# Attention and mixture of experts on one core: regrouping the small loads of the second weights, and phi in longer packets

## The chip, the cores and the metric

The kernel runs on one core of one Trainium2 chip, in one launch. The metric is the device time of that core in microseconds (us), the median of several runs. The core has five engines that run side by side: PE (TensorE, matrix products and transposes), ACT (ScalarE), DVE (VectorE), POOL (GpSimd) and SP (SyncE, which here only issues DMAs). DMAs are issued from the queues of POOL, SP and ACT and are carried out by 16 DMA engines. SBUF is the on-chip memory of 128 partitions, PSUM the small memory that PE writes to.

## The reference

The program is a sliding-window attention followed by a soft mixture of experts. Cut to what matters:

```python
# attention: 8 batches, 8 heads, 576 positions, head size 64
scores = (q @ k.T) / 8
mask_plain = (rel >= 0) & (rel < 32)                         # heads 0-3
mask_dil = (rel >= 0) & (rel < 128) & (rel % 4 == 0)         # heads 4-7
attn = softmax(where(mask, scores, -1e9)); x = attn @ v      # -> 4608 tokens x 512
# soft mixture of experts: phi 512 x 32, w1 8 x 512 x 1024, w2 8 x 1024 x 512
logits = x @ phi                                             # 4608 x 32 slots
d = softmax(logits, over tokens); slot_input = d.T @ x       # 32 slots, 4 per expert
for e in range(8):
    h = relu(slot_input[e] @ w1[e])
    slot_out[e] = h @ w2[e]
c = softmax(logits, over slots); out = c @ slot_out          # 4608 x 512
```

All inputs and the output are float32 in HBM.

## The kernel before

**Units.** The attention is done in eight units, u = 0 to 7, each of one pair of batches and one half of the heads (dilated for even u, plain for odd u). A unit's q, k and v are loaded by `load_unit` into one of three buffers, `stg[:, u % 3]`, of 9,216 bfloat16 columns: q in partitions 0 to 31, k in 32 to 63, v in 64 to 95. Even units take three DMAs that write 32 adjacent partitions each, odd units six that write every second partition of 32. `st_T` turns the unit round by PE transposes into `TT` (two buffers), `st_S` makes the scores and their exponentials, `st_V` and `st_P` multiply with v and normalize into `XB`, `st_X` transposes `XB` into `XT` (L767, six transposes of 96 x 128 for each half x of the 256 columns of a head kind), and `st_L` makes the logits with phi (`phi_pad`, which is cast from `phi_st`) and adds up the slots' inputs.

**Weights.** Weights are cast from float32 to bfloat16 by the loading DMA, all from POOL's queue. `home` gives each expert matrix a place: w1 of experts 0 to 6 in `WD`; w1 of expert 7 and w2 of expert 0 in `stg[:, 2]`, w2 of experts 1 and 2 in `stg[:, 0]`, of experts 3 and 4 in `stg[:, 1]`, each in 4,096 columns, the second of a buffer from column 4096 on; w2 of experts 5 to 7 in `TT`. A weight can be loaded when the attention has finished with the buffer. One expert's w2 takes 4,096 columns in each of 128 partitions: 16 KB of float32 in HBM for a row, 8 KB of bfloat16 in SBUF.

**The loads in question.** Experts 1 and 2 come in one DMA of all 128 rows (`wload2`, L495). For experts 3 and 4, `wpair` issues seven DMAs over both experts: rows 0, 2, 4 ... 126; rows 1, 9, 17 ... 41; rows 49 and 57; rows 65, 73 ... 105; rows 113 and 121; rows 5, 13 ... 125; and rows 3, 7, 11 ... 127. [...] Behind them in the queue come expert 5 (`wload("w25")`), a memset of `hTT` by POOL, and experts 6 and 7 in seven parts, cut into halves of the columns.

**The end.** When the attention is through, the slots' inputs are folded, the first products (`pe` with `siT`) and the second (`ffn2`) run, the second half by half as weights land: `ffn2` takes experts 0 to 3 in its first call, 4 to 6 in part in the next, and 6 and 7 last, first for output columns 0 to 255, then for 256 to 511. `half` makes the output of 1,536 tokens for each half of the columns and stores it in pieces; after it the other tokens follow in four larger stores. Output is staged in the weights' places in `WD` and `stg[:, 2]`.

**Order.** `Prog.schedule` orders the work of all engines by planned times, cost estimates and keys (`DUE`); operations of POOL and of SP keep the order in which the program lists them. `Prog.emit` then writes each engine's list with its semaphore waits. A buffer's `Buf` object keeps who wrote and read it, and `b.parts` which DMA brings which part of a weight, so that a product waits for the parts that it reads.

**phi.** SP issues the load of phi at the start, behind an early load of part of w1: `phi_st` is 128 partitions x 4 x 32 float32, and partition p takes rows p, 128 + p, 256 + p and 384 + p of phi, 128 bytes each.

Of the kernel before, what the change touches and what calls it, by code (L numbers as in the profile page):

```python
# [25 lines left out]
QB = 96  # L26
# [30 lines left out]
class Op:  # L57
    n = 0
# [58 lines left out]
class Prog:  # L117
# [6 lines left out]
    def op(self, e, fn, r=(), w=(), a=(), alloc=(), cost=0.5, key=0.0, mode="f",  # L124
           sem=None, nbytes=0, after=(), ndma=1, n=0, port=False):
        o = Op(e, fn, cost, key, mode)
        deps = list(after)
        for b in r:
            deps += b.ready
        for b in w:  # L130
            b.fresh()
            deps += b.prev
        for b in a:
            deps += b.prev
        seen = set()
        for d in deps:
            if d.id not in seen:
                seen.add(d.id)
                o.deps.append(d)
        for b in r:  # L140
            b.reads.append(o)
        for b in list(w) + list(a):
            b.ready.append(o)
        o.wr = [b for b in list(w) + list(a) if b.pool is not None]
        for b in list(r) + list(w) + list(a):
            if b.pool is not None and b not in o.touch:
                b.left += 1
                o.touch.append(b)
        o.alloc = list(alloc)
        o.sems = sem  # L150
        o.bytes = nbytes
        o.ndma = ndma
        o.n = 2 * n
        o.port = port
        self.ops.append(o)
        return o
# [171 lines left out]
def bass_dilated_sliding_attn__then__soft_moe_slots_kernel(  # L328
# [12 lines left out]
    op = P.op  # L341

    def sb(name, shape, dt=BF16):
        return A(nc.sbuf_tensor(name, shape, dt))
# [3 lines left out]
    WD = sb("WD", [128, 7, 4096])  # L348
    stg = sb("stg", [128, 3, 9216])
# [11 lines left out]
    ident = sb("ident", [128, 128])  # L361
# [4 lines left out]
    phi_st = sb("phi_st", [128, 4, N_SLOTS], F32)  # L366
# [26 lines left out]
    def tile(pool, size=1):  # L393
        t = Buf(pool)
        t.size = size
        return t
# [5 lines left out]
    def sbt(t):  # L402
        return t.pool.ts[t.phys[0]]
# [7 lines left out]
    def bankb(t):  # L411
        return psb[:, t.phys[0], :]
# [5 lines left out]
    b_stg = [Buf() for _ in range(3)]  # L418
# [7 lines left out]
    def due(u, x):  # L426
        return u * DUE["pace"] + x

    def kind(u):
        return 1 - u % 2  # L430
# [23 lines left out]
    HOME = {}  # L454
    b_home = []

    def home(ap, al, name):
        b = Buf()
        b.al = al
        b.parts = []  # L460
        HOME[name] = (ap, b)
        b_home.append((ap, b))
# [24 lines left out]
    def wload2(na, nb):  # L487
        (ap, ba), (_, bb) = HOME[na], HOME[nb]
        e = int(na[2:])
        src = (moe_w1 if na[:2] == "w1" else moe_w2)[e:e + 2].rearrange("e (p c) f -> p e (c f)", p=128)  # L490
        dst = WD[:, e:e + 2, :] if na[:2] == "w1" else stg[:, 0, 0:8192].rearrange("p (e f) -> p e f", e=2)
        pb = Buf()
        for al in ba.al + bb.al:
            pb.prev = pb.prev + al.ready + al.reads
        o = op("pool", lambda g: [g.dma_start(dst, src)], after=pb.prev, a=[pb], cost=0.8,  # L495
               sem=DmaSem(nc, f"s_{na}_{nb}"), nbytes=4194304)
        for b in (ba, bb):
            b.parts.append((0, 8, 0, 512, pb))
            b.ready.append(o)
# [4 lines left out]
    for i, s in enumerate((2, 0, 1)):  # L504
        for h_ in range(2):
            nm = ("w17", "w20", "w21", "w22", "w23", "w24")[2 * i + h_]
            home(stg[:, s, 4096 * h_:4096 * h_ + 4096], [b_stg[s]], nm)
    TTf = TT[:].rearrange("p a x -> p (a x)")
    for i in range(3):
        home(TTf[:, 4096 * i:4096 * i + 4096], b_TT, f"w2{5 + i}")  # L510
# [5 lines left out]
    op("sp", lambda e: [e.dma_start(  # L516
        pre, moe_w1[0].rearrange("(p c) f -> p (c f)", c=4)[:, 0:2048])],
       w=[b_pre], cost=0.1, sem=DmaSem(nc, "s_pre"), nbytes=1048576)
    op("sp", lambda e: [e.dma_start(phi_st[:], moe_phi.rearrange("(c p) s -> p c s", p=128))],
       w=[b_phist], cost=0.1, sem=s_phi, nbytes=65536)  # L520
    op("dve", lambda g: g.memset(id0[:], 0.0), w=[b_id0], cost=0.3)
    op("pool", lambda g: g.affine_select(out=id0[:], in_=id0[:], compare_op=AluOp.not_equal,
# [60 lines left out]
    def blocked(u):  # L583
        return u > 0 and kind(u) == 0
# [170 lines left out]
    def st_X(u, bpar, x):  # L755
        bp, ty = u // 2, kind(u)
        b = 2 * bp + bpar
        px = tile(psum, 1)
        al = [px]
        if x == 0:  # L760
            XT[b, ty] = tile(pXT)
            al.append(XT[b, ty])
        xt, xb = XT[b, ty], XB[b, ty]

        def pe(t):
            for m in range(6):
                i_ = t.transpose(bankb(px)[:, QB * m:QB * m + QB],  # L767
                                 sbt(xb)[:, m, 128 * x:128 * x + 128], ident[0:QB, 0:QB])
            return i_
        k0 = due(u, DUE["X"] + DUE["Xb"] * bpar + 0.8 * x)  # L770
        op("pe", pe, r=[b_id, xb], w=[px], alloc=al, cost=0.31, n=6, key=k0)

        def ev(en):
            d, s_ = sbt(xt)[:, x, :], bankb(px)[:, 0:S]
            if ty:
                s_ = s_.rearrange("p (y x s) -> p s x y", y=2, x=2)
                d = d.rearrange("p (s x y) -> p s x y", y=2, x=2)
            if en is nc.vector:
                return en.tensor_copy(d, s_)
            return en.activation(d, s_, ACTF.Copy)  # L780
        op(("dve", "act"), ev, r=[px], **{"w" if x == 0 else "a": [xt]},
           cost={"dve": 0.38 if ty == 0 else 0.8, "act": 0.57}, key=k0 + 0.6)
# [59 lines left out]
            return i_  # L842
        op("pe", pe3, r=[et, xb0, xb1], a=[b_acc, t_acc], cost=0.35, n=12, mode="c", key=k0 + 4.0)

    mk = sb("mk", [15, 5, 2, 4])
    turns = []

    def turn(n):
        i = len(turns)
        turns.append(n)  # L850
        op("pool", lambda g: [g.dma_start(
            mk[0:n, i, :, 0:2],
            moe_w2[7, 0:n, :].rearrange("p (a x) -> p a x", a=4)[:, 0:2, 0:2])],
           w=[Buf()], cost=0.3, sem=DmaSem(nc, f"s_turn{i}"), nbytes=256)

    def wpair(na, nb, s_, steps):
        e0 = int(na[2:])
        bs = [HOME[na][1], HOME[nb][1]]
        v_ = moe_w2[e0:e0 + 2].rearrange("e (p c) f -> p e (c f)", c=8)
        d_ = stg[:, s_, 0:8192].rearrange("p (e f) -> p e f", e=2)  # L860
        for n, st in enumerate(steps):
            if isinstance(st, int):
                turn(st)
                continue
            r0, r1, step = st
            pb = Buf()
            for al in bs[0].al:
                pb.prev = pb.prev + al.ready + al.reads
            src, dst = v_[r0:r1:step], d_[r0:r1:step]
            o = op("pool", lambda g, src=src, dst=dst: [g.dma_start(dst, src)],  # L870
                   after=pb.prev, a=[pb], cost=0.6, sem=DmaSem(nc, f"s_{na}_{n}"),
                   nbytes=32768 * ((r1 - r0 + step - 1) // step))
            for b in bs:
                b.parts.append((0, 8, 0, 512, pb))
                b.ready.append(o)

    W_AFTER = {2: ["w10"], 3: ["w11"], 4: ["w12"], 5: ["w13"], 6: ["w14"]}
    for u in range(NU):
        for j in range(4):
            st_T(u, j)  # L880
        if u + 3 < NU:
            for n_ in W_AFTER.get(u + 2, ()):
                wload(n_, ((4, 8, 0, 512),) if n_ == "w10" else ((0, 8, 0, 512),))
            load_unit(u + 3)
        else:
            if u == 5:
                wload2("w15", "w16")
                wload("w17")
                wload("w20")
            if u == 6:  # L890
                wload2("w21", "w22")
            if u == 7:
                wpair("w23", "w24", 1, (
                    (0, 128, 2), 15, (1, 49, 8), 2, (49, 65, 8), 6, (65, 113, 8), 2,
                    (113, 128, 8), 7, (5, 128, 8), (3, 128, 4)))
        if u + 1 < NU and blocked(u + 1):
            interleave(u + 1)
        for i in range(6):
            st_S(u, i)
        for g in range(4):  # L900
            st_V(u, g)
        for g in range(4):
            st_P(u, g)
        for bpar in range(2):
            for x in range(2):
                st_X(u, bpar, x)
        if u % 2:
            for bpar in range(2):
                st_L(u - 1 + bpar, u)
# [79 lines left out]
    COLS, d_ = [], 0  # L989
# [3 lines left out]
    for x in range(2):  # L993
        def rsum(t, x=x):
# [5 lines left out]
           cost=0.8, key=K1 + x, after=[ffn1] if x else [])  # L1000
    op("dve", lambda vv: vv.reciprocal(rtok[:], bank(rs)[:, 0:N_TOK // 128]), r=[rs], w=[b_rtok],
       cost=0.2, key=K1 + 1)
# [200 lines left out]
```

## Time and profile before

| | us |
|---|---|
| Median of three runs | 175.43 (175.20 to 175.62) |
| The profiled execution, its own time | 175.14 |
| Its span, first to last instruction | 173.9 |
| PE busy | 127.0 (73%) |
| DVE busy | 113.8 (65%) |
| ACT busy | 95.9 (55%) |
| POOL busy | 62.8 (36%) |
| Mean granted TensorE clock | 0.929 of full speed |
| DMA packets | 12,517, 41.28 MB |

The profile is of one execution. Times are us from the start of the span. Its page has the busy time of each engine, the span in 40 equal slices (a digit is the busy share of a slice in tenths, 9 is 90% or more; the DMA row is the mean over the 16 DMA engines, and the GB/s row is what they moved), the DMA queues, the chain of waits that ended last, the costliest groups of instructions, and the DMA issues with their time from issue to landing. "L495" is line 495 of the kernel; a name like `stg<-in_moe_w_dram` is destination and source. A DMA's issue on POOL is an instruction of its own; the transfer goes on after it.

### The profile page before, as it was taken

The page shows a single profiled execution, that of the slowest core. Times are in us where ns is not written, and L with a number is a line of the kernel's source. Part 1 is how long each engine was busy: PE and PEld are TensorE (multiplying, and loading weights), DVE is VectorE, ACT ScalarE, POOL GpSimd, SP SyncE. Part 2 cuts the span into 40 slices and gives each one's busy share as a digit, 9 for nine tenths or more (in the row PEclk, how much of TensorE's full clock was granted, in tenths as well). Part 3 has the DMA queues.
Part 4 walks back from the last instruction along what each step waited for, and adds up shares of the span by engine and source line. Part 5 has one row for each costly group of instructions (what it writes and reads, how often), then busy time and mean ns, then how long its engine had stood idle before and what let it go on. Part 6 is the DMA issues. An engine that isn't in the chain of part 4 may idle for free.

```text
span 173.9 us, 5097 instructions
## 1 busy us (share of the span) xinstructions
PE 127.0 (73%) x2235; PEld 97.3 (56%) x2235; DVE 113.8 (65%) x259; ACT 95.9 (55%) x147; POOL 62.8 (36%) x106
## 2 busy tenths in 40 slices
PE   0003778987889999979899799987879896599000
PEld 0003758976678877858787688666553533353000
DVE  6960079769978899886979978999430301489400
ACT  2310791789868878776888587674301101589300
POOL 6950199500996006762001756809700000000000
PEclk9999996999999999999999999999975999969755
DMA  5999999999999999998999999999999999999998
GB/s 170 273 208 197 218 231 196 215 212 214 228 212 207 216 214 209 245 212 189 219 214 216 213 215 220 213 215 219 213 211 209 206 197 196 294 358 396 422 433 351
DMA packets 12517, 41.28 MB, mean 237 GB/s; under 512 B 2128, under 2 KB 8784, under 8 KB 9040
## 3 DMA queue, kind: packets, MB, share of 16 engines
q0 software_dynamic: 7952, 30.41, 86.9%
q1 hardware_dynamic: 2912, 8.98, 13.3%
q10 hardware_dynamic: 1632, 1.57, 2.7%
q8 instruction: 17, 0.28, 0.6%
q14 instruction: 4, 0.03, 0.0%
HBM read 61.93 MB, written 9.44 MB: 410 GB/s over the span
## 4 chain that ended last, share of the span: by engine, by line
PE 35%; DMA 23%; DVE 21%; ACT 7%; POOL 4%; issue 3%
DMA TT<-in_moe_w_dram 15%; DMA stg<-in_v_dram 8%; PE ps L641 7%; PE ps L635 6%; DVE XB L750 6%; PE ps L710 6%; DVE PT L700 4%; PE ps L685 4%; ACT TT L667 3%; PE ps L739 3%; PE ps L794 3%; POOL TT L481 3%; PE ps L767 3%; DVE WD L1058 3%; ACT PT L692 3%
## 5 line engine op out<-in xcount | busy, mean ns | idle before, releaser
L692 ACT ACTIVATE PT<-ps 128x768 bf16<-128x768 f32 x48 | 37.0, 815 | 12.0 <-PE ps L685 11.9
L667 ACT ACTIVATE TT<-ps 128x864 f32<-128x864 f32 x32 | 27.5, 896 | 17.3 <-PE ps L641 11.1
L750 DVE TENSOR_TENSOR XB<-ps,RV 96x768 bf16<-96x768 f32 x32 | 30.1, 945 | 0.5
L641 PE MATMUL ps<-ident,stg 96*128 96x96 bf16 x288 | 15.8, 218 | 16.1 <-DMA stg<-in_v_dram 15.8
L715 DVE COPY VN<-ps 128x768 bf16<-128x768 bf16 x32 | 17.2, 544 | 13.1 <-PE ps L710 12.9
L641 PEld LDWEIGHTS ps<-ident,stg 96*128 96x128 bf16 x288 | 14.4, 105 | 16.9 <-DMA stg<-in_v_dram 15.8
L685 PE MATMUL ps<-TT 64*128 64x96 bf16 x384 | 15.6, 204 | 4.9 <-ACT PT L692 2.3
L739 PE MATMUL ps<-VN,PT 128*128 128x65 bf16 x384 | 17.5, 195 | 2.2 <-issue 1.1
L710 PE MATMUL ps<-ident,TT 128*128 128x128 bf16 x192 | 16.5, 226 | 2.0 <-DVE VN L715 0.8
L608 POOL COPY stg<-stg 96x576 f32<-96x576 f32 x24 | 16.4, 684 | 1.5
L1059 ACT ACTIVATE WD<-ps,rtok 128x256 f32<-128x256 f32 (+1 forms) x22 | 10.5, 553 | 11.6 <-PE ps L1076 10.4
L739 PEld LDWEIGHTS ps<-VN,PT 128*128 128x128 bf16 x384 | 14.7, 99 | 3.2 <-issue 1.1
L685 PEld LDWEIGHTS ps<-TT 64*128 64x128 bf16 x384 | 9.6, 94 | 10.1 <-ACT PT L692 3.9
L710 PEld LDWEIGHTS ps<-ident,TT 128*128 128x128 bf16 x192 | 11.6, 101 | 4.8 <-issue 2.0
L700 DVE TENSOR_TENSOR PT<-PT,mask_d 128x768 bf16<-128x768 bf16 x24 | 14.1, 620 | 0.0
L448 POOL DMA_DIRECT2D stg<-in_q_dram x8 | 4.1, 519 | 26.9 <-PE ps L641 26.9
L767 PE MATMUL ps<-ident,XB 96*128 96x96 bf16 x192 | 11.2, 206 | 1.8 <-DVE XB L750 1.6
L700 DVE TENSOR_TENSOR PT<-PT,mask_p 128x768 bf16<-128x768 bf16 x24 | 12.4, 543 | 0.1
L635 PE MATMUL ps<-ident,stg 96*128 96x96 bf16 x216 | 10.5, 206 | 1.0 <-issue 1.0
L780 ACT ACTIVATE XT<-ps 128x576 bf16<-128x576 bf16 x16 | 9.9, 651 | 1.7 <-PE ps L767 1.7
L767 PEld LDWEIGHTS ps<-ident,XB 96*128 96x128 bf16 x192 | 9.0, 98 | 3.1 <-DVE XB L750 2.6
L635 PEld LDWEIGHTS ps<-ident,stg 96*128 96x128 bf16 x216 | 9.7, 98 | 1.6 <-issue 1.1
(98 smaller groups left out, 206.9 us busy)
## 6 DMA issues: line engine op xcount, KB each, us to landing
WD<-in_moe_w_dram POOLq DMA_DIRECT2D x4, 1024.0 KB, 25.0
stg<-in_moe_w_dram POOLq DMA_DIRECT2D x3, 1024.0 KB, 30.3
stg<-in_q_dram POOLq DMA_DIRECT2D x4, 576.0 KB, 18.0
stg<-in_k_dram POOLq DMA_DIRECT2D x4, 576.0 KB, 20.1
stg<-in_v_dram POOLq DMA_DIRECT2D x4, 576.0 KB, 22.7
stg<-in_q_dram POOLq DMA_DIRECT2D x8, 288.0 KB, 17.4
stg<-in_k_dram POOLq DMA_DIRECT2D x8, 288.0 KB, 19.2
stg<-in_v_dram POOLq DMA_DIRECT2D x8, 288.0 KB, 21.1
```

The lines of the kernel that those rows point to most:

```text
L608: return g.tensor_copy(o_, i_)
L635: i_ = t.transpose(bankb2(pt, a)[:, 96 * kk:96 * kk + 96], il_ap(u, j, a)[:, 128 * kk:128 * kk + 128], ident[0:96, 0:96])
L641: i_ = t.transpose(bankb2(pt, a)[:, 96 * kk:96 * kk + 96], two[:, c, :], ident[0:96, 0:96])
L667: return ac.activation(d, sv, ACTF.Copy)
L685: i_ = t.matmul(pair(sc)[:, hx, QB * x:QB * x + QB], win(u, 1, h01, blk_, bpar)[64 * hx:64 * hx + 64], win(u, 0, h01, blk_, bpar)[64 * hx: ...
L692: op("act", lambda ac: ac.activation(sbt(pt)[:, 0:768].rearrange("p (x n) -> p x n", x=2), pair(sc)[:, :, 0:384], ACTF.Exp, scale=SCALE), ...
L700: return dv.tensor_tensor(p_, p_, m.unsqueeze(1).to_broadcast([128, 2, 384]), AluOp.mult)
L710: i_ = t.transpose(bankb(pv)[:, 128 * m:128 * m + 128], win(u, 2, h01, m, bpar), ident[:, :])
L715: op("dve", lambda dv: dv.tensor_copy(sbt(vn)[:, :, :, 0:64], bankb(pv)[:, 0:768].rearrange("p (m x d) -> p m x d", m=6, x=2)), r=[pv], w= ...
L739: i_ = t.matmul(pair(po)[:, bk, 65 * po_:65 * po_ + 65], sbt(pts[i])[:, o_:o_ + 128], sbt(vn)[:, m, half, 0:65], start=True, stop=True)
L750: op("dve", lambda dv: dv.tensor_tensor(sbt(xb)[:].rearrange("p m (x h d) -> p h x m d", x=2, h=2)[:, h01], pv()[:, :, :, 0:64], sbt(rv)[: ...
L767: i_ = t.transpose(bankb(px)[:, QB * m:QB * m + QB], sbt(xb)[:, m, 128 * x:128 * x + 128], ident[0:QB, 0:QB])
```

## The change

**Loads.** The thirteen DMAs become nine. `wrows(e0, n, r0, r1)` loads rows r0 to r1 - 1 of n experts from e0 on in one DMA. In order: experts 1 and 2, rows 16 to 127 (in the place of the full load); experts 3 and 4, rows 16 to 127; experts 1 and 2, rows 8 to 15; experts 3 and 4, rows 8 to 15; a `turn` of 15; experts 1 to 4, rows 0 to 5; a `turn` of 2; experts 1 to 4, rows 6 and 7; a `turn` of 7. Bytes and destinations' rows are the same in sum. So that one DMA can reach four experts with one step, the second expert of each `stg` buffer begins at column 4608 in the place of 4096.

**phi.** Partition p of `phi_st` now takes rows 2p and 2p + 1, and 256 + 2p and 256 + 2p + 1, 256 bytes in one piece each. To match, the transposes of `XB` take every second column (`x::2`) in the place of 128 adjacent ones.

```diff
     def wload2(na, nb):
         ...
-        src = (moe_w1 if na[:2] == "w1" else moe_w2)[e:e + 2].rearrange("e (p c) f -> p e (c f)", p=128)
-        dst = WD[:, e:e + 2, :] if na[:2] == "w1" else stg[:, 0, 0:8192].rearrange("p (e f) -> p e f", e=2)
+        src = moe_w1[e:e + 2].rearrange("e (p c) f -> p e (c f)", p=128)
+        dst = WD[:, e:e + 2, :]
...
-            home(stg[:, s, 4096 * h_:4096 * h_ + 4096], [b_stg[s]], nm)
+            home(stg[:, s, 4608 * h_:4608 * h_ + 4096], [b_stg[s]], nm)
...
-    op("sp", lambda e: [e.dma_start(phi_st[:], moe_phi.rearrange("(c p) s -> p c s", p=128))],
+    op("sp", lambda e: [e.dma_start(phi_st[:].rearrange("p (t x) s -> p t (x s)", x=2), moe_phi.rearrange("(t p x) s -> p t (x s)", p=128, x=2))],
...
-                                 sbt(xb)[:, m, 128 * x:128 * x + 128], ident[0:QB, 0:QB])
+                                 sbt(xb)[:, m, x::2], ident[0:QB, 0:QB])
...
-    mk = sb("mk", [15, 5, 2, 4])
+    mk = sb("mk", [15, 3, 2, 4])
...
-    def wpair(na, nb, s_, steps):
-        ...
+    w2r = moe_w2.rearrange("e (p c) f -> p e (c f)", c=8)
+    stgr = stg[:, 0:2, :].rearrange("p s (h f) -> p (s h) f", h=2)
+
+    def wrows(e0, n, r0, r1):
+        bs = [HOME[f"w2{e0 + i}"][1] for i in range(n)]
+        pb = Buf()
+        for b in bs:
+            for al in b.al:
+                pb.prev = pb.prev + [x for x in al.ready + al.reads if x not in pb.prev]
+        src, dst = w2r[r0:r1, e0:e0 + n], stgr[r0:r1, e0 - 1:e0 - 1 + n, 0:4096]
+        o = op("pool", lambda g: [g.dma_start(dst, src)], after=pb.prev, a=[pb], cost=0.6,
+               sem=DmaSem(nc, f"s_w{e0}_{n}_{r0}"), nbytes=16384 * n * (r1 - r0))
+        for b in bs:
+            b.parts.append((0, 8, 0, 512, pb))
+            b.ready.append(o)
...
             if u == 6:
-                wload2("w21", "w22")
+                wrows(1, 2, 16, 128)
             if u == 7:
-                wpair("w23", "w24", 1, (
-                    (0, 128, 2), 15, (1, 49, 8), 2, (49, 65, 8), 6, (65, 113, 8), 2,
-                    (113, 128, 8), 7, (5, 128, 8), (3, 128, 4)))
+                wrows(3, 2, 16, 128)
+                wrows(1, 2, 8, 16)
+                wrows(3, 2, 8, 16)
+                turn(15)
+                wrows(1, 4, 0, 6)
+                turn(2)
+                wrows(1, 4, 6, 8)
+                turn(7)
```

More of the change, by code (lines that the diff above doesn't have):

```diff
@@ L854, in turn @@
            w=[Buf()], cost=0.3, sem=DmaSem(nc, f"s_turn{i}"), nbytes=256)
-    def wpair(na, nb, s_, steps):
[L857 to L875, printed above, removed]
+    w2r = moe_w2.rearrange("e (p c) f -> p e (c f)", c=8)
[12 more added lines that the diff above has]
+            b.ready.append(o)
     W_AFTER = {2: ["w10"], 3: ["w11"], 4: ["w12"], 5: ["w13"], 6: ["w14"]}
```

## The prediction

> **What bounds the kernel now.** I read the page's second and fourth parts first, since they say whether one resource is full from end to end.
>
> ```profile
> DMA  5999999999999999998999999999999999999998
> GB/s 170 273 208 197 218 231 196 215 212 214 228 212 207 216 214 209 245 212 189 219 214 216 213 215 220 213 215 219 213 211 209 206 197 196 294 358 396 422 433 351
> ...
> HBM read 61.93 MB, written 9.44 MB: 410 GB/s over the span
> ...
> PE 35%; DMA 23%; DVE 21%; ACT 7%; POOL 4%; issue 3%
> ```
>
> The DMA row is nine tenths or more in 38 of 40 slices, while no compute engine passes 73%. The GB/s row counts what lands in SBUF; loads turn float32 into bfloat16 on the way, so 215 landed are 430 read. The fourth part gives DMA only 23%, but it follows waits of instructions, and a wait on a buffer that was free in time hides the transfer behind it. So I asked next for the chain of waits in order of time, late in the kernel.
>
> ```profile
> 119.81 4.35 POOL TT L481 x6
> 124.16 26.64 DMA TT<-in_moe_w_dram
> 150.80 0.04 issue
> ```
>
> The last weights are issued at 124 and land at 150.8. A 26.6 us trip is a backlog in the queue, and nothing on the engines shortens it. Pool's timeline shows how early the loads of the change are issued.
>
> ```profile
> 91.20 0.71 POOL L495 DMA_DIRECT2D stg<-in_moe_w_dram  x1 [8.94 <-PE ps L641]
> ...
> 105.95 0.61 POOL L870 DMA_DIRECT2D stg<-in_moe_w_dram  x1 [3.52 <-PE ps L635]
> 106.55 0.59 POOL L851 DMA_DIRECT2D mk<-in_moe_w_dram  x1
> ...
> 111.53 1.07 POOL L870 DMA_DIRECT2D stg<-in_moe_w_dram  x2
> 117.21 0.57 POOL L481 DMA_DIRECT2D TT<-in_moe_w_dram  x1 [4.62 <-PE ps L710]
> ```
>
> Then a table by stage: us, five engines, granted clock, DMA share, GB/s.
>
> ```profile
> 104.00:126.00 22.00, 18.99 (x373) 15.07 (x371) 17.86 (x43) 12.94 (x23) 14.39 (x21) 1.00 1.03 216
> 126.00:131.00 5.00, 3.70 (x32) 2.62 (x36) 1.42 (x4) 0.28 (x2) 0.00 (x0) 0.77 1.05 208
> 131.00:135.40 4.40, 4.40 (x48) 1.63 (x44) 0.00 (x0) 0.60 (x1) 0.00 (x0) 0.50 1.02 210
> ...
> 150.80:173.90 23.10, 9.57 (x40) 4.26 (x40) 10.48 (x16) 10.02 (x20) 0.00 (x0) 0.69 0.99 391
> ```
>
> The DMA share is 0.99 to 1.05 in each, in the store stage too. The end is the start plus all DMA work; a microsecond of DMA work added or saved anywhere moves it by a microsecond.
>
> **Where the changed loads stand.** Issue time plus time to landing: the 2 MB load of w21 and w22 lands at 91.20 + 34.8 = 126.0, the 1 MB load of even rows at 105.95 + 25.0 = 130.95, the last small one at 112.06 + 23.3 = 135.4, w25 at 117.21 + 23.0 = 140.2. After these come only w26, w27 and the stores, all behind them in full queues.
>
> **Fewer DMAs.** Four fewer issues of 0.56 us take 2.2 us off Pool between 106 and 112.6; Pool then idles 4.62 us for PE before w25, so this is worth nothing. In the queue: from 126.0 to 140.2 land 2,097 + 1,049 KB, 221 GB/s, no less than the 216 of the large loads before. By that a small DMA costs nothing. The tiny loads into mk land 0.2 us after the load ahead of them (106.55 + 24.6 = 131.15 against 130.95), so at most 0.2 each, 0.8 for four. I take 0.1, near the rate of the whole stretch, which includes the small loads.
>
> **phi.** Its 64 KB go in 512 packets of 128 bytes, then in 256 of 256. It lands at 1.25 + 6.7 = 7.95, the SP load ahead of it at 0.81 + 6.5 = 7.3. It costs at most that 0.65 us, so half the packets save 0 to 0.33. I take 0.1, since the bytes stay.
>
> **Strided transposes.** L767 will load every second column of XB as weights. L710 already reads every second column of TT: 98 ns median for a weight load, as L767 (98) and L635 (98) with adjacent ones. Nothing; were it 3 ns more on 192, 0.6 us of PE, under the DMA backlog. The new column offset of w20, w22 and w24 changes no shape: nothing.
>
> **Later waits.** Rows 0 to 15 of w21 and w22 now come after most of w23 and w24. The first FFN2 group needs all four experts anyway, and starts at 138.4, 3.0 us after 135.4. If that cover goes, w25 to w27 behind it are as late and still set the end.
>
> **Where the bytes land.** This decides. Each row of an expert is 8,192 bytes in one partition. The strided loads of before spread rows over all 128 partitions. Now rows 8 to 15 of four experts come in two successive loads, 262 KB into eight adjacent partitions, and rows 0 to 7 in two more, another 262 KB into the eight below. At the queue's 214 GB/s each half takes 1.22 us and nothing is lost. The narrowest stretch that the trace shows is 32 adjacent partitions, in the q, k and v loads (KB each, us to landing):
>
> ```profile
> stg<-in_q_dram POOLq DMA_DIRECT2D x1, 576.0 KB, 17.9
> stg<-in_k_dram POOLq DMA_DIRECT2D x1, 576.0 KB, 19.9
> stg<-in_v_dram POOLq DMA_DIRECT2D x1, 576.0 KB, 22.4
> ```
>
> Issued at 8.84, 9.35 and 9.85 they land at 26.7, 29.25 and 32.25: k and v are 1,180 KB in 5.5 us, 214 GB/s, or 6.7 GB/s for each partition of the stretch. Nothing in the trace goes beyond that. If it is the most a stretch takes, eight partitions take 53.6 GB/s: 262 KB need 4.9 us in place of 1.22, +3.7. The 288 KB loads write every second partition of 32 at the same 210 GB/s, 13 GB/s for a written partition; by these eight take 105 GB/s, 2.5 us, +1.25. Bounds for rows 8 to 15: 0 to +3.7, and the same again for rows 0 to 7. For rows 8 to 15 I take +3.7, because the new rows are adjacent like those of k and v and all queues pass through these two loads. For rows 0 to 7 I take 0: six and then two rows can hold up at most eight of the 16 DMA engines if a row goes through one, and the others go on with w25.
>
> [...]
>
> **Sum.** +3.7 - 0.1 - 0.1 = +3.5 us. The profiled execution took 175.14 (span 173.9 and 1.24 around it), 0.29 below the median 175.43 of the three runs: 178.6.
>
> **Rivals.**
> *Partitions don't matter* (chance 0.28): the small loads run at the queue's 214 GB/s. For it: 32 and 128 partitions run alike, so no limit has shown yet. Against: four times the density. Then only the small savings stay, 0 to -0.4 on 175.4: 175.0 to 175.4, mostly within what a measurement can tell, which is about 0.2% or 0.35 us.
> *Each DMA costs its landing step* (0.1, the case on the other side): with no limit by partitions, four DMAs at 0.2 and phi at its 0.33 give -1.1, 174.3. It decides if the first case holds and landing steps are engine time; the 221 GB/s of the stretch speaks against it. [...]
> *The whole price* (0.12): rows 0 to 7 hold up everything as well, +7.3 - 0.2: 182.2.
> *Half the price* (0.15): the density that counts is by written partition, or DMA engines reach these loads at different times: +1.25 to +2.5, about 177.
> The forecast has 0.35. That a part does nothing is possible for phi alone, if its packets stay at 128 bytes: 0.1 us.
>
> **Numbers.** Slower: 0.35 + 0.12 + 0.15 = 0.62. The first rival's 0.28 is split at the bound of 0.2%, 0.18 the same and 0.1 faster; with the second, faster 0.2. The slower cases' own range is 176.5 to 182.2; with the first rival the 8-in-10 range is 174.9 to 180.6.
>
> **What would show it.** Right: between the 112-row loads and w25 the GB/s falls well below 200 for 4 to 8 us, the last TT load lands near 154 in place of 150.8, and the stores after it take the same 23 us. The time to landing of the eight-row loads lies over 2 us apart from one to the next. Wrong: that stretch still moves 210 GB/s and the last load lands at 150.5 to 150.8; then partitions don't matter. A fall of packets under 512 B by about 256 and of 64 or so tiny ones would show phi and the four DMAs gone, whatever the time.

## The result, and the profile after

The changed kernel takes 177.67 us (median of six runs, 177.29 to 178.32) against 175.31 for the kernel before on the same chip. The ratio is 1.013, 95% interval 1.0098 to 1.0161: slower by 2.3 us (1.7 to 2.8). Here and below a price in microseconds is the ratio less one, times 175.4; the ratios leave disturbed runs out, so they are not in every case exactly the quotient of two medians. The profiled execution took 177.52 us with a span of 176.2.

The page of the changed kernel, the rows that answer to those shown of before:

```profile
DMA  5999998999999999998999999999999999999998
GB/s 169 280 205 203 234 217 185 221 217 215 234 222 192 217 211 214 235 222 189 222 213 210 218 216 214 218 218 214 214 197 114 192 193 197 279 354 394 441 416 357
DMA packets 12165, 41.28 MB, mean 234 GB/s; under 512 B 1776, under 2 KB 8432, under 8 KB 8688
```

The DMA row is as full as before. The GB/s row is too, but for one place: the 31st slice, 132 to 137 us, shows 114 where the kernel before shows 209. That one slice is 95 x 4.4 = 420 KB short, 2.0 us of transfer at 209 GB/s, and the slices on either side of it are 14 GB/s short each, another 0.6 us. The bytes are the same 41.28 MB. Packets under 512 bytes were 2,128 and are 352 fewer: 256 of them are phi's and 96 belong to the new list of loads, as the two kernels below that have one half of the change each show (1,872 and 2,032). The prediction had some 64 for the latter.

The chain of waits in order of time, around the last weights:

```profile
119.09 4.35 POOL TT L481 x6
123.44 29.74 DMA TT<-in_moe_w_dram
153.18 0.04 issue
```

The last weights were issued 0.7 us earlier than before and land 2.4 us later, at 153.18 in place of 150.80. What follows them takes 176.2 - 153.2 = 23.0 us, as before (23.1). So all of the loss lies ahead of 153 us.

Pool's timeline of the changed kernel, and then the rows of DMA issues (KB each, us to landing), each from a window around one or two of these issues:

```profile
90.74 0.68 POOL L866 DMA_DIRECT2D stg<-in_moe_w_dram  x1 [9.38 <-PE ps L641]
...
105.21 1.79 POOL L866 DMA_DIRECT2D stg<-in_moe_w_dram  x3 [2.93 <-PE ps L635]
...
109.22 0.58 POOL L851 DMA_DIRECT2D mk<-in_moe_w_dram  x1
116.48 0.58 POOL L481 DMA_DIRECT2D TT<-in_moe_w_dram  x1 [6.67 <-PE ps L710]
```

```profile
stg<-in_moe_w_dram POOLq DMA_DIRECT2D x1, 1792.0 KB, 29.7
...
stg<-in_moe_w_dram POOLq DMA_DIRECT2D x2, 128.0 KB, 31.1
...
mk<-in_moe_w_dram POOLq DMA_DIRECT2D x1, 0.1 KB, 29.6
...
TT<-in_moe_w_dram POOLq DMA_DIRECT2D x1, 1024.0 KB, 26.1
```

The second load of 112 rows lands at 105.21 + 29.7 = 134.9. The x3 of the second timeline row are this load and the two of eight rows, issued 0.6 apart, so those two land near 105.8 + 31.1 = 136.9 and 106.4 + 31.1 = 137.5. The last of the small loads, a `turn` (a few bytes into the tile `mk`, which nothing reads; the thirteen DMAs before have five of them, the nine of the change three), lands at 109.22 + 29.6 = 138.8, where before the last was at 135.4: 3.4 us later (the last one with weights in it lands at 138.6, 3.2 later). But w25 lands at 116.48 + 26.1 = 142.6 against 140.2, only 2.4 later. About one microsecond was given back between the two: the 1,049 KB of w25 in 3.8 us would be 276 GB/s, well above the 214 of the queue, so a part of w25 had passed while the small loads were still under way. The table by stage shows where the time is lost (us, five engines, granted clock, DMA share, GB/s):

```profile
126.00:131.00 5.00, 4.20 (x40) 2.72 (x36) 0.98 (x3) 0.28 (x2) 0.00 (x0) 0.76 1.08 223
131.00:135.40 4.40, 4.40 (x70) 2.42 (x63) 0.75 (x2) 0.60 (x1) 0.00 (x0) 0.88 1.26 123
135.40:140.20 4.80, 1.95 (x24) 1.06 (x26) 0.74 (x4) 0.48 (x3) 0.00 (x0) 0.86 0.98 167
...
153.20:176.20 23.00, 8.66 (x40) 3.52 (x40) 10.32 (x16) 10.08 (x20) 0.00 (x0) 0.78 1.00 392
```

Between 131.0 and 135.4 the rate is 123 GB/s in place of 210, and in the very same stretch the DMA share is 1.26, where it was 1.02. The DMA engines aren't idle there: they hold packets that take longer. By the packets of the two traces that start in that stretch, one of 8 KB took 1.20 us on average (66 of them, the longest 1.85), where before it took 0.63 (113). The next row is low too, 167 GB/s where it was 203. The loads ahead of these two rows and the stores behind run as before.

### The profile page after: what moved, and what is told of

Read it like the earlier page. It is cut to its first block, busy times and chain, and to the rows that moved or that the text cites. A ratio compares the mean times of both kernels' runs of the same rounds, so it can differ in the third digit from the quotient of the medians.

```text
span 176.2 us, 5092 instructions
## 1 busy us (share of the span) xinstructions
PE 127.2 (72%) x2235; PEld 97.3 (55%) x2235; DVE 114.1 (65%) x259; ACT 95.9 (54%) x147; POOL 61.0 (35%) x102
## 2 busy tenths in 40 slices
DMA packets 12165, 41.28 MB, mean 234 GB/s; under 512 B 1776, under 2 KB 8432, under 8 KB 8688
## 4 chain that ended last, share of the span: by engine, by line
PE 30%; DMA 24%; DVE 19%; ACT 13%; POOL 4%; issue 3%; ACTq 0%
DMA TT<-in_moe_w_dram 17%; DMA stg<-in_v_dram 7%; DVE XB L750 7%; PE ps L641 6%; PE ps L635 6%; DVE PT L700 5%; PE ps L710 5%; ACT WD L1059 4%; ACT TT L667 3%; PE ps L685 3%; ACT PT L692 3%; DVE VN L715 3%; PE ps L767 3%; POOL TT L481 3%; PE ps L739 2%
## 5 line engine op out<-in xcount | busy, mean ns | idle before, releaser
L641 PEld LDWEIGHTS ps<-ident,stg 96*128 96x128 bf16 x288 | 14.7, 106 | 16.3 <-DMA stg<-in_v_dram 15.1
L1059 ACT ACTIVATE WD<-ps,rtok 128x256 f32<-128x256 f32 (+1 forms) x22 | 10.5, 553 | 16.0 <-PE ps L1076 14.8
L700 DVE TENSOR_TENSOR PT<-PT,mask_d 128x768 bf16<-128x768 bf16 x24 | 14.8, 650 | 0.0
L1058 DVE TENSOR_SCALAR so_sb<-ps,rcs 128x256 bf16<-128x256 f32 x2 | 1.0, 484 | 14.6 <-PE ps L1024 14.6
```

Of the source, the lines that this page charges most:

```text
L641: i_ = t.transpose(bankb2(pt, a)[:, 96 * kk:96 * kk + 96], two[:, c, :], ident[0:96, 0:96])
L700: return dv.tensor_tensor(p_, p_, m.unsqueeze(1).to_broadcast([128, 2, 384]), AluOp.mult)
L1059: return en.activation(d_, s_, ACTF.Copy, scale=k_)
```

## The experiments

Two readings of the loss were set against each other at first: that it comes from which partitions the small loads write, or from something else in the new list of loads (their number, their order, phi). Later the first was split in two: a limit by the stretch of partitions that is written (called A1), or paths into SBUF, with partitions 32 apart on the same path (A2), a guess until the runs with larger loads below. Where a list of loads is shown, it is the whole of what the kernel issues for w21 to w24; `wrows(e0, n, r0, r1)` loads rows r0 to r1 - 1 of n experts from e0, and a fifth argument, added for these runs, is a step in rows.

**Phi alone: no effect.** The kernel before, with phi's two edits and nothing else:

```diff
-    op("sp", lambda e: [e.dma_start(phi_st[:], moe_phi.rearrange("(c p) s -> p c s", p=128))],
+    op("sp", lambda e: [e.dma_start(phi_st[:].rearrange("p (t x) s -> p t (x s)", x=2), ...)],
...
-                                 sbt(xb)[:, m, 128 * x:128 * x + 128], ident[0:QB, 0:QB])
+                                 sbt(xb)[:, m, x::2], ident[0:QB, 0:QB])
```

> The kernel before with phi in 256-byte packets and the strided transposes of XB alone. Theory A (the small loads of the change write too few adjacent partitions at a time, and that rate is the price): nothing of the +2.3 us is here, 0 to -0.3 us against before. Rival C (phi or the strided transposes cost the time, by PE or at the start): +2 us or more, as the whole change.

Measured: 175.35 against 175.36, ratio 1.0006 [0.998, 1.0032]. The 256 packets saved and the strided weight loads of the transposes are worth nothing that can be measured.

**The loads alone: the whole loss.** The changed kernel with phi's two edits undone, that is, the diff above in reverse.

> The nine loads and the new column offset alone, phi and the transposes as before. Theory A, and rival B (the eight-row loads use only eight DMA engines each and leave the engines unevenly loaded, whatever the partitions): +2.2 to +2.6 us against before, the whole change. Rival C: 0.

Measured: 177.72 against 175.36, ratio 1.0136 [1.0106, 1.0167]; +2.4 us. The whole of the 2.3 is in the loads.

**The same bytes in the same number of DMAs, dense or spread.** Two kernels with six loads each, in the same order and of the same sizes: two of 96 rows, then four of 16 rows. They differ only in which 16 of the 32 rows a small load takes.

```diff
 # every second row of 32                  # 16 adjacent rows
 wrows(1, 2, 32, 128)                      wrows(1, 2, 32, 128)
 wrows(3, 2, 32, 128)                      wrows(3, 2, 32, 128)
-wrows(1, 2, 0, 32, 2)
-wrows(3, 2, 0, 32, 2)
-wrows(1, 2, 1, 32, 2)
-wrows(3, 2, 1, 32, 2)
+                                          wrows(1, 2, 0, 16)
+                                          wrows(3, 2, 0, 16)
+                                          wrows(1, 2, 16, 32)
+                                          wrows(3, 2, 16, 32)
```

> As the changed kernel, but rows 0 to 31 of both pairs come in four loads of 16 rows each, every second partition (even rows of each pair, then odd rows), behind loads of rows 32 to 127; no loads into mk, so the evening-out of the DMA engines is gone. Theory A: 16 rows over a stretch of 32 partitions are what the odd units' loads write at 210 GB/s, so no price for partitions: the last w25 lands near 140.2, total 175.0 to 176.3 (the upper end if the lost evening-out costs up to 1 us). Rival B: the same, since all 16 engines have the same work. Rival D (any load into few partitions at a time is slow): 177 or more.

> As the run with every second row of 0 to 31, with the same number and size of loads, but adjacent rows: rows 0 to 15 of each pair, then rows 16 to 31. Theory A: 16 adjacent partitions at 6.7 GB/s each take 107 GB/s, so the 1,049 KB need up to 9.8 us in place of 4.9; with engines that arrive at different times +2 to +4.9 us over the run with every second row. Theory A' (13 GB/s for each written partition, wherever it lies) and rival B: the same time as that run, within 0.4 us.

Measured, every second row: 175.85 against 175.36, ratio 1.0019 [0.9992, 1.0045]. Adjacent rows: 180.2, ratio 1.0267 [1.0226, 1.0308]. The stride alone is worth 180.2 - 175.85 = 4.35 us. The table by stage of the first and of the second, in the same two stretches:

```profile
132.00:134.00 2.00, 2.00 (x39) 0.87 (x32) 0.02 (x1) 0.60 (x1) 0.00 (x0) 1.00 1.08 221
134.00:136.00 2.00, 1.61 (x26) 1.47 (x25) 1.40 (x5) 0.48 (x3) 0.00 (x0) 1.00 1.02 213
```

```profile
132.00:134.00 2.00, 2.00 (x36) 0.91 (x32) 0.00 (x0) 0.60 (x1) 0.00 (x0) 0.83 1.20 152
134.00:136.00 2.00, 2.00 (x39) 1.48 (x28) 0.82 (x2) 0.00 (x0) 0.00 (x0) 1.00 1.03 123
```

The DMA share is 1.0 to 1.2 in both; of the two DMA columns only the last tells them apart. This settles that the partitions written are the cause. It also says that 16 rows spread over 32 partitions still run at the full rate.

**The change's own small loads, spread.** Loads of 8, 6 and 2 rows over the same experts in the same order as in the change, with the three tiny `turn` loads between them, but of every fourth row; the large part is split for it, so there are 13 DMAs.

```diff
-wrows(1, 2, 16, 128)
+wrows(1, 2, 0, 128, 2); wrows(1, 2, 1, 128, 4); wrows(1, 2, 67, 128, 4)
-wrows(3, 2, 16, 128)
+wrows(3, 2, 0, 128, 2); wrows(3, 2, 1, 128, 4); wrows(3, 2, 67, 128, 4)
-wrows(1, 2, 8, 16); wrows(3, 2, 8, 16); turn(15)
+wrows(1, 2, 3, 35, 4); wrows(3, 2, 3, 35, 4); turn(15)
-wrows(1, 4, 0, 6); turn(2); wrows(1, 4, 6, 8); turn(7)
+wrows(1, 4, 35, 59, 4); turn(2); wrows(1, 4, 59, 67, 4); turn(7)
```

> The changed kernel with the same small loads in the same order (two of 8 rows, one of 6 and one of 2 rows over four experts, the three loads into mk between them), but on every fourth partition of 0 to 63 in the place of the adjacent rows 0 to 15; the other rows come in three loads for each pair (64, 32 and 16 rows). Theory A (adjacent partitions share a rate): the price is gone, 175.0 to 175.8. Rival B (loads of 8, 6 and 2 rows leave the DMA engines unevenly loaded): 177.6, as the change.

Measured: 175.36 against 175.32, ratio 1.0001 [0.9973, 1.0029]. The loss is gone, with loads over four experts and of eight rows still there. Its chain of waits has the last weights back at 125.51 + 25.27 = 150.8, the microsecond at which the kernel before has them:

```profile
125.51 25.27 DMA TT<-in_moe_w_dram
```

**No small loads at all: what eleven DMAs are worth.**

```diff
+wrows(1, 2, 0, 128)
+wrows(3, 2, 0, 128)
```

> The changed kernel with two whole loads of 128 rows for experts 1 to 4, no small loads and none into mk: two DMAs, not nine. It tells what the small loads and the evening-out are worth. If eleven DMAs fewer than before save 0.2 us each: 173.2. If they cost nothing and the evening-out is worth what the run with every second partition lost (175.85 against 175.36): 175.6 to 176.2.

Measured: 175.83 against 175.32, ratio 1.0032 [1.0012, 1.0051]. With 11 fewer DMAs than before the kernel is 0.6 us slower, not faster. Spread small loads alone don't win this back: the kernel with every second row has four of them and is no faster than this one. Both are without `turn` loads, and two more kernels without them, further down, have a slack end: with blocks 32 apart the DMA share is 0.90 from 158 to 160 us, and the last weights land at 161.10; with blocks 16 apart it is 0.88 from 150 to 152, and they land at 153.28. With `turn` loads it is 1.38 from 148 to 150 in the kernel before, where they land at 150.80, and 1.43 from 150 to 152 in the changed kernel, where they land at 153.18. These are the rows from 150 to 152 of the changed kernel and of the one with blocks 16 apart:

```profile
150.00:152.00 2.00, 1.87 (x20) 1.26 (x17) 1.68 (x3) 1.63 (x5) 0.00 (x0) 1.00 1.43 210
```

```profile
150.00:152.00 2.00, 1.83 (x20) 1.23 (x17) 1.67 (x3) 1.63 (x5) 0.00 (x0) 1.00 0.88 173
```

So the `turn` loads may earn the 0.6. No run changes them alone, so neither this nor how they would do it is shown.

**Eight rows, sixteen or four apart: not told apart.** If partitions 32 apart share a path, rows 3, 19, 35, ... 115 share theirs with others of the same load, while of rows 3, 7, 11, ... 31 no two are 32 apart.

```diff
 wrows(1, 2, 0, 128, 2); wrows(1, 2, 1, 128, 4)    # and the same of experts 3 and 4
+wrows(1, 2, 7, 128, 8)       # sixteen apart;     four apart: wrows(1, 2, 67, 128, 4)
+wrows(1, 2, 3, 128, 16)      # of both pairs;     wrows(1, 2, 3, 35, 4)
+wrows(1, 2, 11, 128, 16)     # of both pairs;     wrows(1, 2, 35, 67, 4)
```

> Small loads of 8 rows again, four of them with no loads into mk, on partitions 3, 19, 35 ... 115 (both pairs), then 11, 27 ... 123 (both pairs): spread over all 128 partitions. Theory A1 (what counts is the stretch that a load covers): no price, the same time as the run with every fourth partition of a stretch of 32, within 0.4 us. [...]

> As the run with rows 16 apart, same number and size of loads, but on every fourth partition of 3 to 31, then of 35 to 63. A1 and A2 both: no price for partitions, 175.2 to 176.2, where the lost evening-out makes the upper end. Rival B: 177 or more here and in the run with rows 16 apart alike.

Measured: sixteen apart 1.0061 [1.0034, 1.0088], four apart 1.0047 [1.0024, 1.0069]. The intervals overlap nearly whole, and in both tables by stage all four stretches from 130 to 138 us show 201 to 217 GB/s. Both kernels are without `turn` loads, as is the kernel without small loads with its +0.6; theirs are +1.1 and +0.8 us. The difference between them that A2 asks for didn't show, so this pair speaks against A2 as I had it, or the loads are too short for it: DMA engines may reach them at different times, with few inside at once, which no run here shows. Larger loads had to decide.

**Larger loads, 32 or 16 apart.** Both kernels issue eight loads: 16 rows and 80 rows of each pair, then four of 16 rows, which write two blocks of 16 partitions in turn. In one kernel the two blocks lie 32 partitions apart, in the other 16.

```diff
 # 32 apart                                # 16 apart
-wrows(1, 2, 16, 32)                       wrows(1, 2, 32, 48)
 wrows(1, 2, 48, 128)                      wrows(1, 2, 48, 128)
-wrows(3, 2, 16, 32)                       wrows(3, 2, 32, 48)
 wrows(3, 2, 48, 128)                      wrows(3, 2, 48, 128)
 wrows(1, 2, 0, 16)                        wrows(1, 2, 0, 16)
-wrows(3, 2, 32, 48)                       wrows(3, 2, 16, 32)
 wrows(3, 2, 0, 16)                        wrows(3, 2, 0, 16)
-wrows(1, 2, 32, 48)                       wrows(1, 2, 16, 32)
```

> Loads of 16 adjacent rows again, no loads into mk. First rows 16 to 31 and 48 to 127 of each pair, then at the end, one behind the other, rows 0 to 15, 32 to 47, 0 to 15 and 32 to 47 of the two pairs. Theory A1 (each stretch of adjacent partitions has its own rate): two different stretches take turns, so the price is smaller than with the same stretch twice in a row, and equal to that of the run with rows 16 to 31 in the place of 32 to 47, within 0.5 us. Theory A2 (partitions 32 apart are on the same path): all four loads, 1,049 KB, go over the same paths, so the whole price of the run with adjacent rows is here, 180 to 181 us, and 1.5 to 3 us more than in the run with rows 16 to 31. [...]

> The same as the run with stretches 32 apart, with the same number, size and order of loads, but rows 0 to 15 and 16 to 31 take turns at the end, and rows 32 to 47 and 48 to 127 come first. A1: as that run, within 0.5 us. A2: the two stretches are on different paths, so two loads that overlap don't share: 177 to 179 us, 1.5 to 3 us less than that run.

Measured: 32 apart 185.0 against 175.8, ratio 1.0506 [1.0415, 1.0598]; 16 apart 177.48, ratio 1.0101 [1.0063, 1.0138]. That is +8.9 and +1.8 us, 7.1 between them, for the same sizes and number of loads. The tables by stage, 32 apart first:

```profile
116.00:118.00 2.00, 1.77 (x40) 1.40 (x38) 2.00 (x5) 1.26 (x2) 0.00 (x0) 1.00 1.09 115
118.00:120.00 2.00, 1.85 (x41) 1.57 (x42) 2.00 (x6) 1.75 (x4) 0.00 (x0) 1.00 0.95 164
...
134.00:136.00 2.00, 2.00 (x24) 0.78 (x20) 0.00 (x0) 0.06 (x1) 0.00 (x0) 0.50 1.04 102
136.00:138.00 2.00, 2.00 (x24) 0.71 (x20) 0.00 (x0) 0.60 (x1) 0.00 (x0) 0.50 1.09 107
138.00:140.00 2.00, 2.00 (x32) 0.76 (x24) 0.04 (x1) 0.00 (x0) 0.00 (x0) 0.76 1.18 119
140.00:142.00 2.00, 1.57 (x26) 1.44 (x24) 1.42 (x5) 0.48 (x3) 0.00 (x0) 1.00 1.02 102
```

```profile
116.00:118.00 2.00, 1.54 (x35) 1.15 (x36) 2.00 (x4) 1.19 (x3) 0.82 (x2) 1.00 1.04 217
118.00:120.00 2.00, 1.67 (x33) 1.30 (x29) 1.93 (x6) 1.00 (x2) 2.00 (x2) 1.00 1.05 221
...
134.00:136.00 2.00, 2.00 (x38) 1.11 (x31) 0.43 (x1) 0.01 (x1) 0.00 (x0) 0.98 1.16 184
136.00:138.00 2.00, 1.19 (x19) 1.05 (x18) 1.06 (x5) 0.48 (x3) 0.00 (x0) 1.00 0.94 184
138.00:140.00 2.00, 1.41 (x28) 0.85 (x32) 0.00 (x0) 0.00 (x0) 0.00 (x0) 1.00 1.01 202
```

Blocks 32 apart pass at 102 to 119 GB/s for eight microseconds, no faster than loads into one block (152 and 123 above); blocks 16 apart pass at 184 to 202, with 152 only from 132 to 134. A limit by stretch would have it the other way round, or alike: 0 to 15 and 32 to 47 are no denser than 0 to 15 and 16 to 31. So A1 falls, and A2 stands for these blocks. What a path is, and whether and how many adjacent partitions share one, no run here shows.

The difference is more than the 1.5 to 3 us I had expected, and the rows say where some of it is. Between 116 and 120 us the first kernel also has a dip that the second hasn't: rows 16 to 31 stand ahead of rows 48 to 127 in the queue, and 48 to 63 are 32 above 16 to 31, so by the same reading they share their paths too. In the second kernel the 16 rows ahead are 32 to 47, and no dip shows (217 and 221). I hadn't counted that.

**Rows 0 to 15 in one load: half the bytes of the dense kernel.** Two loads of 112 rows and one of rows 0 to 15 over all four experts. The dense kernel is the one with 16 adjacent rows above.

```diff
+wrows(1, 2, 16, 128)
+wrows(3, 2, 16, 128)
+wrows(1, 4, 0, 16)
```

> Three loads for experts 1 to 4: rows 16 to 127 of each pair, and one load of rows 0 to 15 over all four experts, 524 KB into 16 adjacent partitions, half of what the run with adjacent rows put into narrow stretches. Theory A: half of its price of 4.35 us over the run with two whole loads (175.83): about 178.0. If the price comes only with several narrow loads in a row: 175.8. If it hangs on the number of loads: a quarter, 176.9.

Measured: 179.18 against 175.8, ratio 1.021 [1.0137, 1.0282]; +3.7 us (2.4 to 4.9) where 178.0 was expected. Half of the dense kernel's 4.35, with the 0.6 that the kernel without small loads lacks, would be 2.8: inside the interval, so the dose isn't shown to be out of proportion. What it does show is that nine, six and three DMAs, over two or four experts, all lose time as soon as the rows are adjacent.

**The change's loads in another order.** The nine DMAs of the change, unaltered, but each load of rows 8 to 15 right behind the load of 112 rows of its own pair, so that the two are issued some 14 us apart.

```diff
             if u == 6:
                 wrows(1, 2, 16, 128)
+                wrows(1, 2, 8, 16)
             if u == 7:
                 wrows(3, 2, 16, 128)
-                wrows(1, 2, 8, 16)
                 wrows(3, 2, 8, 16)
                 turn(15)
                 ...
```

> The changed kernel with its nine DMAs and all sizes as they are, in another order: the load of rows 8 to 15 of each pair stands right behind the load of rows 16 to 127 of the same pair, so that the two loads into these eight partitions are some 9 us apart in the queue and not one behind the other. [...] If the order doesn't matter (a fixed price of each narrow load): 177.7, as the change.

Measured: 176.78 against 175.65, ratio 1.0056 [1.0024, 1.0088]; +1.0 us in place of +2.3. Its table by stage has one low stretch where the change has three (135, 90 and 135 GB/s between 132 and 138 us):

```profile
132.00:134.00 2.00, 2.00 (x24) 0.76 (x20) 0.00 (x0) 0.48 (x1) 0.00 (x0) 0.50 1.21 185
134.00:136.00 2.00, 2.00 (x28) 0.68 (x20) 0.00 (x0) 0.12 (x1) 0.00 (x0) 0.65 1.08 131
136.00:138.00 2.00, 1.88 (x30) 1.60 (x26) 1.16 (x3) 0.32 (x3) 0.00 (x0) 1.00 1.06 217
```

The order alone is worth 1.3 us of the 2.3 (0.5 to 2.1 by the two intervals): that is the price of two loads into the same eight partitions following each other. That other engines write elsewhere meanwhile, when large loads stand between them, is the likely reason and isn't shown by itself.

## Why the prediction was right, and where it was off

**What bounds the kernel: right.** The end moved by 2.4 us because the queue did, and the stores after it took 23.0 us as before. In the kernel with blocks 32 apart the last weights land at 161.1 and 23.0 us follow, so the same chain carries a loss of 8.9 us to the end. One reading of it was too narrow: the DMA share is 0.99 to 1.05 in each row that the prediction shows, but from 140.2 to 150.8 us it is 1.40 at 215 GB/s.

**Fewer DMAs and phi, -0.1 each: both nothing.** Phi alone is 1.0006 with zero inside its interval, and 11 fewer DMAs gained nothing. The rival that each DMA costs its landing step (174.3) is dead: with 11 of them gone, 0.2 us each would have given -2.2, and +0.6 was measured.

**Strided transposes and later waits at nothing: borne out.** Phi's kernel has the same transposes at no cost. The later waits never came to set the end: in all kernels the chain goes through parts of w26 or w27. In the kernel without small loads and in the one with loads pulled apart it is an earlier part of these, landing at 146.85 and 147.87, with products behind it.

**Where the bytes land: right in kind, its size off.** The term for rows 8 to 15 was +3.7. The small loads do end 3.4 us late. The total is +2.3 and not +3.5 because the term was carried to the end unchanged: a part of w25 passed beside the small loads, which the sum granted for rows 0 to 7 and not for rows 8 to 15, and 1.0 us was won back before w25 landed. By the order of the loads the pair of rows 8 to 15 measured between 1.3 us (what pulling them apart saves) and the whole 2.3. The eight-row loads weren't over 2 us apart, as I had said they would be: they landed 2.0 and 0.6 us after the load ahead of each. That fits DMA engines that come to them at different times, so that both loads are under way together. The half-price rival named this, as one of its two reasons, at about 177. The result of 177.67 lies between it and the forecast of 178.6. The sum starts from the profiled execution's 175.14; from the median of 175.43 it would be 178.9. That all queues pass through these two loads, one reason for taking the whole +3.7, was an assumption: no trace here shows which engine carries which row.

**The unit was wrong where the number was right.** I took 6.7 GB/s for each partition of a stretch from the k and v loads, which write 32 adjacent partitions at 214 GB/s. By the blocks 32 and 16 apart it isn't the stretch but the paths: if 16 adjacent partitions take 102 to 119 GB/s, as the blocks 32 apart did, 32 take some 204 to 238 (an estimate: twice that; the blocks 16 apart passed at 184 to 202). So by this estimate k and v ran just at the rate at which the queue delivers anyway, and that this row lay near a limit was a coincidence. It is luck that the unit came out right. It also fits that every second of 32 rows was free, at 221 and 213 GB/s. The other estimate, 13 GB/s for a written partition, bounds the measured +2.3 between its +1.25 and +2.5 for the wrong reason: the same number of written partitions cost 4.35 us more as 16 adjacent rows than as every second of 32.

**Rows 0 to 7 at nothing: probably not quite.** With rows 8 to 15 pulled apart 1.0 us (0.4 to 1.5) is left. That is rows 0 to 7 and what a single load of eight adjacent rows costs; the two weren't separated, and this kernel's end is slow as well: 258 GB/s in the 35th slice of its page, where the changed kernel has 279 and the kernel before 294. So the term for rows 8 to 15 was too large and the one for rows 0 to 7 probably too small; the two errors partly cancel, and that the total came within 1 us is in part luck. That rows 0 to 7 hold up at most eight of the DMA engines was an assumption, too, which no run shows.

**What stays open.** Why the loss with blocks 32 apart is larger than their own slow passage: by the 6.7 GB/s for a partition, 107 for 16 (the rows show 102 to 119), the four blocks would cost some +4.9 us at the end of the queue (an estimate: 1,049 KB at 107 in place of 214 GB/s), the dip at 116 to 120 some 1.4 more (2 x 99 + 2 x 50 = 298 KB short of 214 GB/s), 6.3 in all, and 8.9 (7.3 to 10.5) was measured. The table by stage shows the rest without explaining it: the rate stays low longer, 127 from 142 to 144 and 164 from 144 to 146, and there is a second dip from 122 to 126 (193 and 168). In sum that kernel is 1,850 KB short of 214 GB/s from 112 to 150 us, 8.7 us. Open, too, is the pair of loads sixteen and four apart, which by A2 should have differed and didn't.

## What to carry to other kernels

Where the DMA queues are full from end to end, ask of every small load which partitions it writes before counting DMAs: rows spread by a step of two or four kept the full rate here (197 to 225 GB/s from 130 to 138 us), loads into eight or 16 adjacent partitions cost 2.3 to 4.7 us, and 8.9 with their blocks 32 apart. Loads into the same few partitions, or into blocks 32 apart as here, shouldn't follow each other in a queue (1.3 and 7.1 us here). A DMA share near or above 1 (1.26 in the low stretch here) says only that engines hold packets, so read the GB/s beside it (123 there, 210 before): the slice where the one stays and the other halves is the place to look.

## What the runs showed of the hardware that I hadn't expected

Loads into partitions 0 to 15 and 32 to 47 in turn slow each other as if they shared a path into SBUF, and loads into 0 to 15 and 16 to 31 hardly do: 102 to 119 GB/s from 134 to 142 us against 184 to 202 from 134 to 140, 7.1 us of the whole kernel. The recorded DMA share doesn't fall when such loads are slow: 1.26 at 123 GB/s, where it is 1.02 at 210 in the kernel before. And 11 DMAs fewer made the kernel 0.6 us slower, where the prediction had -0.1 for four fewer.
